# Second query group turned on TensorE: products with the identity in place of a VectorE transpose, 128-token query products, and a mask moved ahead of a division

## The chip, the cores and the metric

The kernel runs on one core of a Trainium2 chip. The metric is the device time of one execution in microseconds (us), lower is better. "The time" below is the median of the runs shown unless it says otherwise.

## The reference

Two blocks run one after the other. The first is a linear attention whose features are outer products of two 8-row sketches; the second is a two-layer network with an ELU between the layers.

```python
# q, k, v: (batch 4, heads 4, tokens 1088, 32), float32; S1, S2: (8, 32), float64
def phi(x):                                     # 64 features of a token
    a = einsum('rd,bhsd->bhsr', S1, x); b = einsum('rd,bhsd->bhsr', S2, x)
    return einsum('bhsi,bhsj->bhsij', a, b).reshape(..., 64)
kv  = einsum('bhsf,bhsd->bhfd', phi(k), v);  z = phi(k).sum(tokens)
x   = (phi(q) @ kv) / (phi(q) @ z + 1e-6)       # heads side by side: (4352, 128)
h   = x @ w_in                                  # w_in (128, 2048), float64
out = where(h > 0, h, exp(min(h, 0)) - 1) @ w_out   # w_out (2048, 128), float64
```

The weights arrive as 64-bit floats, and the kernel makes 32-bit floats of their words itself ("rounding" below).

## The kernel before

**Stages.** The 4352 tokens are cut into half tiles of 64; eight half tiles make a group of 512 tokens (groups 0 to 8). Everything up to the first product with `w_in` is the head: the keys of batch 0 are turned and sketched, key features and values are summed into `kv`, and the queries of groups 0 and 1 go through sketch, division (`q2_den`), feature products (`q2_out`), a turn on TensorE (`q4_early`) and the product with `kv` (`q5_early`), which gives `xg`, the network's input. After the head each step is one pair of 128-wide slices of the hidden layer: `mm1` (tile `h`), ELU on ScalarE (`elu_a`: RELU, then EXP) and VectorE (`elu_d`, tile `gg`), then `mm2` (tile `o`, or `pa`/`pb` where a seven-product scheme is used). Keys and queries of later batches are worked into these steps at fixed places.

**Order.** The schedule is written out by hand: each engine runs its instructions in the order in which the program text issues them, and a waiting instruction keeps those behind it on its engine waiting. Each `dma_start` on `nc.sync` goes to SP's queue in the same way.

**Rounding of a weight slice** takes `RA` (a mask on VectorE, L101), `RB` (a RELU with a scale on ScalarE, L106) and `RC` (sign L116, mantissa L120, low word L128, product L136, all on VectorE). Slices 0 and 1 are the two first `w_in` pairs, slices 2 and 3 the two first `w_out` pairs; `RC_2` treats the two `w_in` pairs in one go, and `RE` is its last step.

**Tiles and lines.** `qT` holds the queries of a batch with head dimension on the partitions: `transp` (L281) is one STREAM_TRANSPOSE on VectorE from the loaded tile `hd_q`. Half tiles 0 to 7 of batch 0 are turned first, 8 to 16 later (L974). The products that read it in the head are `q1_first` (tile `abqp`, L516), `q1z_first` (`zqp`, L528; denominators) and `q1_second` (`abwp`, L537; group 1). `KA` (`kv`, L428) sums keys and values; `KS_first` turns its result into `kvS` (L480 to L482). `q4_early` writes `qtp` (L636) and ScalarE copies it to `qpT` (L637); `q5_early` writes `xps` (L643), which ScalarE copies to `xg` (L649). `keep_warm` issues products of ones whose result (`idle`) nobody reads.

**PSUM.** Tag `h` has four banks in turn, tag `aux` two, `o0` and `o1` one each; `kv` of batch 0 lies in `o1`.

The text order just ahead of and behind the first `mm1`:

```python
    q5_early(0)
    keep_warm(1, 192, width[0])
    mm1_first()
    q2(1, 2, lambda: RA(2))
    RB(2)
    elu_a(0, 0, 0)
    elu_a(0, 0, 1, (0,))
    mm1(0, 1, (0,))
    q4_early(1)
```

Of the kernel before, what the change touches and what calls it, by code (L numbers as in the profile page):

```python
# [12 lines left out]
F32 = mybir.dt.float32  # L13
# [9 lines left out]
def _ap(ap: bass.AP, free):  # L23
    return dataclasses.replace(ap, ap=[list(ap.ap[0])] + [list(x) for x in free])
# [3 lines left out]
def kernel(  # L28
# [21 lines left out]
    nc = tc.nc  # L50
    B, H, S, D = q.shape
    R = S1.shape[0]
    P = 128
# [21 lines left out]
    def load_hd(eng, x, src, b, t0, t1, c=slice(0, 2)):  # L75
        if (x, b) not in hd:
            hd[x, b] = work.tile([P, 2, NT, D], F32, name="hd_" + x, tag="hd_" + x)
        eng.dma_start(hd[x, b][:, c, t0:t1, :],
                      src[b].rearrange("h (a c t) d -> (h a) c t d", a=32, c=2)[:, c, t0:t1, :])
# [104 lines left out]
    def RA(i):  # L184
        round_w(round_a, i)

    def RB(i):
        round_w(round_b, i)
# [23 lines left out]

    load_v(0)
    load_w(0, 0)
    load_hd(nc.sync, "q", q, 0, 8, NT)
    load_w(1, 0)
    load_w(1, 1)
    load_w(0, 1)
# [35 lines left out]
    def quarters(dst, lhs, rhs, tile=None, **kw):  # L254
        tile = tile or width[0]
        for c in range(0, P, tile):
            nc.tensor.matmul(dst[c:c + tile], lhs[:, c:c + tile], rhs, skip_group_check=True,  # L257
                             tile_position=(0, c), **kw)


    def keep_warm(n, cols=256, tile=P):
        ones = nc.const_aps.tensor(1.0, [P, 256], F32)
        for i in range(n):
            for c in range(0, P, tile):
                nc.tensor.matmul(idle[c:c + tile, :cols], ones[:, :tile], ones[:, :cols], skip_group_check=True,  # L265
                                 tile_position=(0, c))
# [13 lines left out]
    def transp(dst, x, b, t0, t1):  # L280
        nc.vector.transpose(dst[b][:, t0:t1, :].rearrange("p t (a c) -> p c t a", c=2), hd[x, b][:, :, t0:t1, :])  # L281


    SXh = const.tile([P, FD], F32, name="SXh")

    def make_SXh():
# [9 lines left out]
    SW = const.tile([FD, H, 3, R], F32, name="SW")  # L296
    SWq = const.tile([FD, B, 2, 4, R], F32, name="SWq")
    SWs = const.tile([FD, B - 1, 4, R], F32, name="SWs")
    keep_warm(3)
    keep_warm(1, 224)  # L300
    sps = psum.tile([P, 512], F32, name="sps", tag="aux")
    nc.tensor.matmul(sps[:, :2 * R], Sx[:].rearrange("p h d -> p (h d)"), ident[:, :2 * R])
    make_SXh()
# [119 lines left out]
    def KA(b):  # L423
        kv = kv_ps[b] = psum.tile([P, 512], F32, name="kv", **(dict(tag="aux") if b else dict(tag="o1", bufs=1)))
        kp = [feats.pop((b, half)) for half in range(2)]
        for i in range(KT):
            for h in range(H):
                nc.tensor.matmul(kv[32 * h:32 * h + 32, :R * R], vt[b][:, (h * KT + i) * D:(h * KT + i + 1) * D],  # L428
                                 kp[i // 5][:, i % 5, h].rearrange("p i j -> p (i j)"),
                                 start=(i == 0), stop=(i == KT - 1), skip_group_check=True, tile_position=(0, 32 * h))  # L430
            if b:
                z_tile(b, kv, i)
# [10 lines left out]

    def Z(b, ps, zl):

        quarters(ps[:, 96:128], SXh[:], zl[:], None if b else 64)

    def Z_out(b, ps):
        z = wzs[b] = SW[:, :, 2, :] if b == 0 else work.tile([FD, H, R], F32, name="wz", tag="wz")[:]
# [25 lines left out]
            z_tile(0, ps, i)  # L475
        return ps, ZC(0, ps)

    def KS_first():
        kd = work.tile([P, 2, R * R], F32, name="kd", tag="kd", bufs=1)
        nc.scalar.copy(kd[:], _ap(kv_ps[0][:, :R * R], [[0, 2], [1, R * R]]))  # L480
        nc.tensor.transpose(kv_ps[0][:, 128:256], kd[:].rearrange("p w f -> p (w f)"), ident[:])
        nc.scalar.copy(kvS[:].rearrange("p h d -> p (h d)"), kv_ps[0][:, 128:256])  # L482

# [14 lines left out]
    def half_tile(g, k):  # L498
        return divmod(8 * g + k, NT)
# [11 lines left out]
    def q1_first():  # L511
        p = psum.tile([P, 512], F32, name="abqp", tag="aux")
        for i in range(4):
            for u in range(2):
                b, t = half_tile(0, 2 * i + u)
                nc.tensor.matmul(p[64 * u:64 * u + 64, i * 64:i * 64 + 64], qT[b][:, t, :],  # L516
                                 Sab[:].rearrange("p h y -> p (h y)"),
                                 skip_group_check=True, tile_position=(0, 64 * u))
        abw[0] = work.tile([P, H * 4, 2 * R], F32, name="abq", tag="abq", bufs=1)
        nc.scalar.copy(abw[0][:].rearrange("p (h t) y -> p h t y", h=H),  # L520
                       p[:, :256].rearrange("p (t h y) -> p h t y", t=4, h=H))

    def q1z_first():
        p = psum.tile([P, 512], F32, name="zqp", tag="h", bufs=4)
        for i in range(4):
            for u in range(2):
                b, t = half_tile(0, 2 * i + u)
                nc.tensor.matmul(p[64 * u:64 * u + 64, i * 32:i * 32 + 32].rearrange("p (h r) -> p h r", h=H),  # L528
                                 qT[b][:, t, :], SW[:, :, 2, :], skip_group_check=True, tile_position=(0, 64 * u))
        return p[:, :128].rearrange("p (t h r) -> p h t r", t=4, h=H)  # L530

    def q1_second():
        p = psum.tile([P, 512], F32, name="abwp", tag="h", bufs=4)
        for i in range(4):
            for u in range(2):
                b, t = half_tile(1, 2 * i + u)
                nc.tensor.matmul(p[64 * u:64 * u + 64, i * 96:i * 96 + 96], qT[b][:, t, :],  # L537
                                 SW[:].rearrange("p h x r -> p (h x r)"), skip_group_check=True,
                                 tile_position=(0, 64 * u))
        abw[1] = work.tile([P, H * 4, 3 * R], F32, name="abw1", tag="abq1", bufs=1)  # L540
        nc.scalar.copy(abw[1][:].rearrange("p (h t) y -> p h t y", h=H),
                       p[:, :384].rearrange("p (t h y) -> p h t y", t=4, h=H))
# [49 lines left out]
    def q2(g, parts=1, between=None):  # L592
        q2_den(g, None, between)
        q2_out(g, parts)

    def q2_den(g, zq=None, between=None):
        m = H * (un[g] if g > 1 else qn[g])
        x = abw[g][:, :m, :]
        pw = pws[g % 2]
        if zq is None:  # L600
            nc.vector.tensor_mul(pw[:, :m, :R], x[:, :, R:2 * R], x[:, :, 2 * R:3 * R])
        else:
            nc.vector.tensor_mul(pw[:, :m, :R].rearrange("p (h t) r -> p h t r", h=H),
                                 x[:, :, R:2 * R].rearrange("p (h t) r -> p h t r", h=H), zq)
        if between:
            between()
        den = work.tile([P, 8 * H], F32, name="den", tag="den")
        nc.vector.tensor_reduce(den[:, :m], pw[:, :m], axis=AX, op=ADD)
        nc.vector.reciprocal(den[:, :m], den[:, :m])
        an = work.tile([P, 8 * H, R], F32, name="an", tag="an")  # L610
        nc.vector.tensor_mul(an[:, :m], x[:, :, R:2 * R], _ap(den[:, :m], [[1, m], [0, R]]))
        ans[g] = an

    def q2_out(g, parts=1, between=None):
        m = H * qn[g]
        x, an = abw.pop(g), ans.pop(g)
        qp[g] = work.tile([P, 4 * H, R, R], F32, name="qp", tag="qp", bufs=2)
        for i in range(parts):
            if i and between:
                between()  # L620
            h = slice(i * m // parts, (i + 1) * m // parts)
            a_ = an[:, h]
            b_ = x[:, h, :R]
            nc.vector.tensor_mul(qp[g][:, h], _ap(a_, list(a_.ap[1:]) + [[0, R]]),
                                 _ap(b_, [b_.ap[1], [0, R], b_.ap[2]]))

    def q4_early(g):

        qpT[g] = work.tile([P, H, 2, P], F32, name="qpT", tag="qpT", bufs=2)
        for hh in range(2):  # L630
            p = psum.tile([P, 512], F32, name="qtp", tag="aux")
            for h2 in range(2):
                for m in range(2):
                    o = (h2 * 2 + m) * P
                    r = (2 * hh + h2) * 4 + 2 * m
                    nc.tensor.transpose(p[:, o:o + P], qp[g][:, r:r + 2].rearrange("p t i j -> p (t i j)"), ident[:])  # L636
            nc.scalar.copy(qpT[g][:, 2 * hh:2 * hh + 2], p[:].rearrange("p (h m s) -> p h m s", h=2, m=2))  # L637

    def q5_early(g):
        xp = [psum.tile([P, 512], F32, name="xps", tag="aux") for _ in range(2)]  # L640
# [320 lines left out]
    Z(0, zps, zl)  # L961
    Z_out(0, zps)
    KO_first(7, KT)
    keep_warm(1, 96, 64)
    zq = q1z_first()
    q2_den(0, zq, lambda: RA(0))
    q2_out(0, 2, lambda: RA(1))
    KA(0)
    KS_first()
    keep_warm(1)  # L970
    RB(0)
    RB(1)
    q4_early(0)
    transp(qT, "q", 0, 8, NT)  # L974
    RC_2()
    RE(0)
    RE(1)
    q1_second()
    q5_early(0)
    keep_warm(1, 192, width[0])  # L980
    mm1_first()
    q2(1, 2, lambda: RA(2))
    RB(2)
    elu_a(0, 0, 0)
# [218 lines left out]
```

## Time and profile before

| | us |
|---|---|
| median of 3 runs | 265.75 |
| the 3 runs | 265.44 to 265.97 |
| the profiled execution, its own time | 265.08 |
| its span | 263.3 |
| TensorE busy | 257.8 (98%) |
| VectorE busy | 188.2 (71%) |
| ScalarE busy | 184.5 (70%) |
| GpSimd busy | 168.2 (64%) |
| first product with `w_in` begins | 15.58 |

The granted TensorE clock is 1.0 throughout. TensorE's busy share says that a product is in flight, not that the array is full. The 16 DMA engines are busy from 3 us to about 24 us of the span, at 228 to 405 GB/s in each us, and have little to do after that. Times inside the span are counted from its start; the difference between the span and the execution's own time, 1.78 us, lies around it.

### The profile page before, as it was taken

What the parts mean: (1) busy time and instruction counts of PE and PEld (TensorE: products, weight loads), DVE (VectorE), ACT (ScalarE), POOL (GpSimd) and SP (SyncE); (2) the same over time, 40 slices, a digit from 0 to 9 for tenths busy, and PEclk for the clock granted to TensorE, in tenths of its full rate; (3) what the DMA queues carried; (4) which work ended last, traced back from release to release, by engine and by line L of the source; (5) the groups of instructions that cost most, each with busy time, mean ns of one, the idle gap of its engine ahead of it and who ended that gap; (6) DMA issues with size and microseconds to landing.
All of it is one profiled execution on the core that took longest, in us unless ns stands there. A gap on an engine that the chain in (4) does not pass through costs nothing.

```text
span 263.3 us, 9739 instructions
## 1 busy us (share of the span) xinstructions
PE 257.8 (98%) x4127; PEld 160.5 (61%) x4127; DVE 188.2 (71%) x349; ACT 184.5 (70%) x356; POOL 168.2 (64%) x251
## 2 busy tenths in 40 slices
PE   8899999999999999999999999999999999999994
PEld 7652334354346756667666666665666666667994
DVE  6899999997969997996477676644446445674651
ACT  2479978677567656775587777776777777777793
POOL 4400009105477996798869799888688888998300
PEclk9999999999999999999999999999999999999999
DMA  5997099020011110000100110011001100110011
GB/s 176 339 349 209 2 277 230 1 72 18 2 24 26 26 20 2 2 4 17 31 3 0 29 18 0 2 19 25 3 2 21 23 4 0 18 20 8 2 30 32
DMA packets 26442, 13.73 MB, mean 52 GB/s; under 512 B 19328, under 2 KB 24576, under 8 KB 26400
## 3 DMA queue, kind: packets, MB, share of 16 engines
q1 hardware_dynamic: 25968, 12.76, 18.9%
q8 instruction: 32, 0.52, 0.9%
q10 hardware_dynamic: 368, 0.30, 0.3%
q0 software_dynamic: 64, 0.07, 0.1%
q14 instruction: 10, 0.08, 0.1%
HBM read 10.88 MB, written 2.23 MB: 50 GB/s over the span
## 4 chain that ended last, share of the span: by engine, by line
PE 96%; POOL 1%; DVE 1%; ACT 1%; issue 0%
PE h L257 44%; PE pb L792 16%; PE pa L792 13%; PE o L257 5%; PE pb L768 4%; PE ol L257 3%; PE idle L265 1%; PE kv L428 1%; PE h L686 1%; PE qps L686 1%; POOL kp L324 1%; PE kfps L360 1%; PE qps L576 1%; PE qtp L636 1%; PE kv L257 1%; PE abp L341 1%
## 5 line engine op out<-in xcount | busy, mean ns | idle before, releaser
L257 PE MATMUL h<-xg,W 128*32 128x512 f32 (+3 forms) x904 | 130.7, 539 | 0.4 <-ACT xg L649 0.4
L875 DVE SCALAR_TENSOR_TENSOR gg<-e,h 128x512 f32<-128x512 f32 x128 | 85.6, 683 | 54.1 <-ACT e L869 50.6
L867 ACT ACTIVATE e<-h 128x512 f32<-128x512 f32 x128 | 75.5, 590 | 45.6 <-PE h L257 42.9
L869 ACT ACTIVATE e<-e 128x512 f32<-128x512 f32 x128 | 80.9, 632 | 3.8
L257 PEld LDWEIGHTS h<-xg,W 128*32 128x32 f32 (+1 forms) x904 | 42.6, 122 | 43.2 <-issue 34.9
L754 POOL TENSOR_TENSOR tt<-gg 128x256 f32<-128x256 f32 x50 | 37.0, 741 | 16.4 <-DVE gg L875 16.1
L751 POOL TENSOR_TENSOR tt<-gg 128x256 f32<-128x256 f32 x50 | 36.7, 734 | 5.5 <-DVE gg L875 5.1
L755 POOL TENSOR_TENSOR tt<-tt,gg 128x256 f32<-128x256 f32 x50 | 37.5, 750 | 3.9
L756 POOL TENSOR_TENSOR tt<-gg,tt 128x256 f32<-128x256 f32 x50 | 37.2, 744 | 3.9
L792 PEld LDWEIGHTS pa<-gg,W 128*64 128x64 f32 (+1 forms) x496 | 23.8, 125 | 23.5 <-issue 22.9
L792 PE MATMUL pa<-gg,W 128*64 128x128 f32 (+1 forms) x496 | 30.5, 274 | 0.0
L792 PE MATMUL pb<-tt,SS 128*64 128x128 f32 (+1 forms) x480 | 29.5, 273 | 0.0
L792 PEld LDWEIGHTS pb<-tt,SS 128*64 128x64 f32 (+1 forms) x480 | 22.6, 126 | 0.0
L792 PE MATMUL pa<-tt,SS 128*32 128x128 f32 (+1 forms) x288 | 21.0, 273 | 0.0
L133 POOL TENSOR_TENSOR raw<-raw,tiny 128x512 f32<-128x512 f32 x1 | 1.0, 1044 | 29.4 <-DVE raw L128 29.4
L792 PE MATMUL pb<-tt,W 128*64 128x128 f32 (+1 forms) x256 | 19.8, 273 | 0.0
L792 PE MATMUL pb<-gg,SS 128*64 128x128 f32 (+1 forms) x256 | 19.8, 273 | 0.0
L257 PE MATMUL o<-gg,W 128*32 128x512 f32 x128 | 15.3, 594 | 0.0
L792 PEld LDWEIGHTS pa<-tt,SS 128*32 128x32 f32 (+1 forms) x288 | 13.6, 124 | 0.0
L792 PEld LDWEIGHTS pb<-gg,SS 128*64 128x64 f32 (+1 forms) x256 | 12.7, 125 | 0.0
L792 PEld LDWEIGHTS pb<-tt,W 128*64 128x64 f32 (+1 forms) x256 | 12.6, 125 | 0.0
L768 PE MATMUL pb<-gg,W 128*32 128x256 f32 x192 | 11.5, 380 | 0.0
(163 smaller groups left out, 279.5 us busy)
## 6 DMA issues: line engine op xcount, KB each, us to landing
raw<-in_moe_w_in_dram SPq DMA_DIRECT2D x8, 256.0 KB, 6.6
raw<-in_moe_w_out_dram SPq DMA_DIRECT2D x8, 256.0 KB, 6.4
hd_k<-in_k_dram SPq DMA_DIRECT2D x3, 544.0 KB, 7.3
hd_q<-in_q_dram SPq DMA_DIRECT2D x3, 544.0 KB, 7.9
out_dram<-ob SPq DMA_DIRECT2D x88, 16.0 KB, 1.5
v<-in_v_dram SPq DMA_DIRECT2D x4, 288.0 KB, 6.8
v<-in_v_dram SPq DMA_DIRECT2D x4, 256.0 KB, 8.3
hd_k<-in_k_dram SPq DMA_DIRECT2D x1, 288.0 KB, 3.3
```

The costliest lines, as they stand in the source:

```text
L257: nc.tensor.matmul(dst[c:c + tile], lhs[:, c:c + tile], rhs, skip_group_check=True, tile_position=(0, c), **kw)
L265: nc.tensor.matmul(idle[c:c + tile, :cols], ones[:, :tile], ones[:, :cols], skip_group_check=True, tile_position=(0, c))
L686: nc.tensor.matmul(ps[w][s * r:s * r + s, 64 * k:64 * (k + m)], lhs, qpT[g, i][rows, o + 2 * k:o + 2 * (k + m), f, :], start=(f == 0 and j ...
L751: nc.gpsimd.tensor_tensor(t[:, 0], b12, b11, op=SUB)
L754: nc.gpsimd.tensor_tensor(t[:, 2], b22, b12, op=SUB)
L755: nc.gpsimd.tensor_tensor(t[:, 1], t[:, 2], b11, op=ADD)
L756: nc.gpsimd.tensor_tensor(t[:, 3], b21, t[:, 1], op=SUB)
L768: nc.tensor.matmul(acc[1][0][r:r + width[0], 256 * hi:256 * hi + 256], lhs[:, w:w + width[0]], gg[:, c, 256 * u:256 * u + 256], start=(cp ...
L792: nc.tensor.matmul(bank[r:r + width[0], P * col:P * col + P], lhs[:, w:w + width[0]], rhs[:, u], start=(first and i in ((0,) if g == 1 els ...
L867: nc.scalar.activation(e, hs[g, cp][c][:, :n], RELU, scale=-1.0)
L869: nc.scalar.activation(e, e, EXP, scale=-1.0)
L875: nc.vector.scalar_tensor_tensor(gs[g, cp][:, c, :n], es[g, cp][:, c, :n], -1.0, hs[g, cp][c][:, :n], op0=ADD, op1=MAX)
```

## The change

- The load of half tiles 8 to 16 of batch 0 (one DMA into `hd_q`) becomes two DMAs into a new tile `q2s`, with the tokens on the partitions: half tiles 8 to 11 on partitions 0 to 63, 12 to 16 on 64 to 127.
- The VectorE transpose of these half tiles goes. In its place `turn_q` makes 16 products of `q2s` with the identity (four heads by four), `turn_q_out` copies them to `qT` on ScalarE in two halves, and `turn_q_last` turns the single half tile 16 by four products behind `mm1_first`, with a ScalarE copy.
- `q1_first`, `q1z_first` and `q1_second` use 128 tokens as the stationary operand in place of two times 64; `Z` of batch 0 and one `keep_warm` use 128 columns too. The other `keep_warm` calls change in size or go.
- `RA(0)` stands ahead of the division's first product in place of behind it; `RB(0)` stands ahead of `KA(0)`; `KS_first` is cut in two, and its second half stands between the halves of `q4_early(0)`.

```diff
@@ -212,7 +212,10 @@
     load_v(0)
     load_w(0, 0)
-    load_hd(nc.sync, "q", q, 0, 8, NT)
+    q2s = const.tile([P, H, 5, D], F32, name="q2s")
+    for u, t0, t1 in ((0, 8, 12), (1, 12, NT)):
+        nc.sync.dma_start(q2s[64 * u:64 * u + 64, :, :t1 - t0, :],
+                          q[0].rearrange("h (y t) d -> y h t d", t=NT)[:, :, t0:t1, :])
     load_w(1, 0)
     load_w(1, 1)
     load_w(0, 1)
@@ -259,7 +262,7 @@
     def keep_warm(n, cols=256, tile=P):
-        ones = nc.const_aps.tensor(1.0, [P, 256], F32)
+        ones = nc.const_aps.tensor(1.0, [P, 512], F32)
         for i in range(n):
             for c in range(0, P, tile):
                 nc.tensor.matmul(idle[c:c + tile, :cols], ones[:, :tile], ones[:, :cols], skip_group_check=True,
@@ -281,6 +284,28 @@
         nc.vector.transpose(dst[b][:, t0:t1, :].rearrange("p t (a c) -> p c t a", c=2), hd[x, b][:, :, t0:t1, :])
+    turned_q = []
+    def turn_q(t0, t1):
+        if not turned_q:
+            turned_q.append(psum.tile([P, 512], F32, name="qtu", tag="h", bufs=4))
+        for t in range(t0, t1):
+            for h in range(H):
+                nc.tensor.matmul(turned_q[0][D * h:D * h + D, P * t:P * t + P], q2s[:, h, t, :], ident[:],
+                                 skip_group_check=True, tile_position=(0, D * h))
+    def turn_q_out(t0, t1):
+        nc.scalar.copy(qT[0][:, 8:16, :].rearrange("p (u t) y -> p t u y", u=2)[:, t0:t1],
+                       turned_q[0][:, P * t0:P * t1].rearrange("p (t u y) -> p t u y", u=2, y=64))
+    def turn_q_last():
+        for h in range(H):
+            nc.tensor.matmul(kv_ps[0][D * h:D * h + D, 256:320], q2s[64:, h, 4, :], ident[64:, 64:],
+                             skip_group_check=True, tile_position=(64, D * h))
+        nc.scalar.copy(qT[0][:, 16, :], kv_ps[0][:, 256:320])
     SXh = const.tile([P, FD], F32, name="SXh")
     def make_SXh():
@@ -296,8 +321,7 @@
     SW = const.tile([FD, H, 3, R], F32, name="SW")
     SWq = const.tile([FD, B, 2, 4, R], F32, name="SWq")
     SWs = const.tile([FD, B - 1, 4, R], F32, name="SWs")
-    keep_warm(3)
-    keep_warm(1, 224)
+    keep_warm(2, 496)
     sps = psum.tile([P, 512], F32, name="sps", tag="aux")
     nc.tensor.matmul(sps[:, :2 * R], Sx[:].rearrange("p h d -> p (h d)"), ident[:, :2 * R])
     make_SXh()
@@ -443,7 +467,7 @@
     def Z(b, ps, zl):
-        quarters(ps[:, 96:128], SXh[:], zl[:], None if b else 64)
+        quarters(ps[:, 96:128], SXh[:], zl[:], None if b else P)
     def Z_out(b, ps):
         z = wzs[b] = SW[:, :, 2, :] if b == 0 else work.tile([FD, H, R], F32, name="wz", tag="wz")[:]
@@ -475,9 +499,12 @@
             z_tile(0, ps, i)
         return ps, ZC(0, ps)
-    def KS_first():
+    def KS_first_a():
         kd = work.tile([P, 2, R * R], F32, name="kd", tag="kd", bufs=1)
         nc.scalar.copy(kd[:], _ap(kv_ps[0][:, :R * R], [[0, 2], [1, R * R]]))
+        return kd
+    def KS_first_b(kd):
         nc.tensor.transpose(kv_ps[0][:, 128:256], kd[:].rearrange("p w f -> p (w f)"), ident[:])
         nc.scalar.copy(kvS[:].rearrange("p h d -> p (h d)"), kv_ps[0][:, 128:256])
@@ -511,11 +538,9 @@
     def q1_first():
         p = psum.tile([P, 512], F32, name="abqp", tag="aux")
         for i in range(4):
-            for u in range(2):
-                b, t = half_tile(0, 2 * i + u)
-                nc.tensor.matmul(p[64 * u:64 * u + 64, i * 64:i * 64 + 64], qT[b][:, t, :],
-                                 Sab[:].rearrange("p h y -> p (h y)"),
-                                 skip_group_check=True, tile_position=(0, 64 * u))
+            b, t = half_tile(0, 2 * i)
+            nc.tensor.matmul(p[:, i * 64:i * 64 + 64], qT[b][:, t:t + 2, :].rearrange("p t y -> p (t y)"),
+                             Sab[:].rearrange("p h y -> p (h y)"), skip_group_check=True)
         abw[0] = work.tile([P, H * 4, 2 * R], F32, name="abq", tag="abq", bufs=1)
         nc.scalar.copy(abw[0][:].rearrange("p (h t) y -> p h t y", h=H),
                        p[:, :256].rearrange("p (t h y) -> p h t y", t=4, h=H))
@@ -523,20 +548,18 @@
     def q1z_first():
         p = psum.tile([P, 512], F32, name="zqp", tag="h", bufs=4)
         for i in range(4):
-            for u in range(2):
-                b, t = half_tile(0, 2 * i + u)
-                nc.tensor.matmul(p[64 * u:64 * u + 64, i * 32:i * 32 + 32].rearrange("p (h r) -> p h r", h=H),
-                                 qT[b][:, t, :], SW[:, :, 2, :], skip_group_check=True, tile_position=(0, 64 * u))
+            b, t = half_tile(0, 2 * i)
+            nc.tensor.matmul(p[:, i * 32:i * 32 + 32].rearrange("p (h r) -> p h r", h=H),
+                             qT[b][:, t:t + 2, :].rearrange("p t y -> p (t y)"), SW[:, :, 2, :],
+                             skip_group_check=True)
         return p[:, :128].rearrange("p (t h r) -> p h t r", t=4, h=H)
     def q1_second():
         p = psum.tile([P, 512], F32, name="abwp", tag="h", bufs=4)
         for i in range(4):
-            for u in range(2):
-                b, t = half_tile(1, 2 * i + u)
-                nc.tensor.matmul(p[64 * u:64 * u + 64, i * 96:i * 96 + 96], qT[b][:, t, :],
-                                 SW[:].rearrange("p h x r -> p (h x r)"), skip_group_check=True,
-                                 tile_position=(0, 64 * u))
+            b, t = half_tile(1, 2 * i)
+            nc.tensor.matmul(p[:, i * 96:i * 96 + 96], qT[b][:, t:t + 2, :].rearrange("p t y -> p (t y)"),
+                             SW[:].rearrange("p h x r -> p (h x r)"), skip_group_check=True)
         abw[1] = work.tile([P, H * 4, 3 * R], F32, name="abw1", tag="abq1", bufs=1)
         nc.scalar.copy(abw[1][:].rearrange("p (h t) y -> p h t y", h=H),
                        p[:, :384].rearrange("p (t h y) -> p h t y", t=4, h=H))
@@ -624,7 +647,7 @@
             nc.vector.tensor_mul(qp[g][:, h], _ap(a_, list(a_.ap[1:]) + [[0, R]]),
                                  _ap(b_, [b_.ap[1], [0, R], b_.ap[2]]))
-    def q4_early(g):
+    def q4_early(g, between=None):
         qpT[g] = work.tile([P, H, 2, P], F32, name="qpT", tag="qpT", bufs=2)
         for hh in range(2):
@@ -635,6 +658,8 @@
                     r = (2 * hh + h2) * 4 + 2 * m
                     nc.tensor.transpose(p[:, o:o + P], qp[g][:, r:r + 2].rearrange("p t i j -> p (t i j)"), ident[:])
             nc.scalar.copy(qpT[g][:, 2 * hh:2 * hh + 2], p[:].rearrange("p (h m s) -> p h m s", h=2, m=2))
+            if between and hh == 0:
+                between()
     def q5_early(g):
         xp = [psum.tile([P, 512], F32, name="xps", tag="aux") for _ in range(2)]
@@ -961,24 +986,28 @@
     Z(0, zps, zl)
     Z_out(0, zps)
     KO_first(7, KT)
-    keep_warm(1, 96, 64)
+    keep_warm(1, 96)
     zq = q1z_first()
-    q2_den(0, zq, lambda: RA(0))
+    RA(0)
+    q2_den(0, zq)
     q2_out(0, 2, lambda: RA(1))
+    RB(0)
     KA(0)
-    KS_first()
-    keep_warm(1)
-    RB(0)
+    kd = KS_first_a()
+    turn_q(0, 2)
+    turn_q_out(0, 2)
+    turn_q(2, 4)
+    turn_q_out(2, 4)
     RB(1)
-    q4_early(0)
-    transp(qT, "q", 0, 8, NT)
+    q4_early(0, lambda: KS_first_b(kd))
     RC_2()
     RE(0)
     RE(1)
     q1_second()
     q5_early(0)
-    keep_warm(1, 192, width[0])
+    keep_warm(1, 128)
     mm1_first()
+    turn_q_last()
     q2(1, 2, lambda: RA(2))
     RB(2)
     elu_a(0, 0, 0)
```

## The prediction

> **What bounds the kernel now.** I read the page's chain by engine first, then the chain in order of time through the head, then ScalarE and VectorE alone in the timeline around the first products with `w_in`.
>
> The page's line:
>
> ```profile
> PE 96%; POOL 1%; DVE 1%; ACT 1%; issue 0%
> ```
>
> TensorE carries the end nearly everywhere, so whatever delays TensorE is paid in full unless it had a hole. The chain through the head (start, us, what):
>
> ```profile
> 11.01 0.69 DVE qp L624
> 11.70 0.21 DVE W L101
> 11.91 0.61 DVE qp L624
> ...
> 12.65 0.63 PE qtp L636 x4
> 13.28 0.85 PE abwp L537 x16
> 14.13 0.70 PE xps L643 x16
> 14.83 0.64 ACT xg L649 x2
> ...
> 15.58 2.79 PE h L257 x40
> 18.37 1.02 PE qtp L636 x8
> 19.39 0.99 PE h L257 x8
> 20.39 0.59 PE xps L643 x16
> 20.98 1.85 PE o L257 x16
> ```
>
> The chain sits on VectorE's query rows up to 12.5 us, then goes through the turn, `xps` and `xg` to the first `h` at 15.58, which I call T. From T on it never leaves TensorE. So the change has two accounts: what it does to T, and what it puts behind T. Next, ScalarE from the timeline (start, duration, instruction, idle before and its releaser):
>
> ```profile
> 14.81 0.65 ACT L649 COPY xg<-xps 128x256 f32<-128x256 f32 x2 [0.15 <-PE xps L643]
> 16.21 0.51 ACT L106 ACTIVATE W<-W,ebias 128x256 uint32<-128x256 uint32 x1 [0.75 <-DVE W L101]
> 17.14 0.60 ACT L867 ACTIVATE e<-h 128x512 f32<-128x512 f32 x1 [0.42 <-PE h L257]
> 17.77 0.63 ACT L869 ACTIVATE e<-e 128x512 f32<-128x512 f32 x1
> 18.30 0.58 ACT L867 ACTIVATE e<-h 128x512 f32<-128x512 f32 x1
> 18.99 1.07 ACT L637 COPY qpT<-qtp 128x512 f32<-128x512 f32 x2
> ```
>
> Between T and the first RELU ScalarE does one weight step (RB(2), L106) in its idle time; from 17.14 on it is full. And VectorE:
>
> ```profile
> 9.62 0.29 DVE L603 TENSOR_TENSOR pw<-abq,zqp 128x128 f32<-128x128 f32 x1 [0.23 <-PE zqp L528]
> 9.82 0.33 DVE L101 TENSOR_SCALAR W<-raw 128x256 uint32<-128x256 uint32 x1
> 18.43 0.69 DVE L875 SCALAR_TENSOR_TENSOR gg<-e,h 128x512 f32<-128x512 f32 x1
> 20.30 0.43 DVE L136 SCALAR_TENSOR_TENSOR W<-raw,W 128x256 f32<-128x256 f32 x1
> ```
>
> The last two tell what is late next: `gg` starts 0.03 us behind its EXP, and the rounding of the first `w_out` slice queues behind it and ends at 20.73, just ahead of the first `o` product at 20.91.
>
> **What the Trainium skill says.** "TensorE: Matmul & The Clock Gate", under the architectural detail of the array, gives ScalarE and VectorE strictly first-in-first-out queues, and lets TensorE pull only weight loads ahead, not products. The trace agrees: RB(2) ran ahead of the RELU although it had to wait 0.75 us, as in the text. "TensorEngine Tiling", Key Properties, says that a change of tiling mode drains TensorE. Here 16 `o` products take 1.85 us behind `xps` (another mode) and 1.72 us behind `h` (the same): about 0.13 us a change. "DMA: Bandwidth & Descriptors", Specifications, names 512 B as the least for line rate; the new load's rows are 512 and 640 B, the old ones 1152 B. No row here shows such a load.
>
> **Part 1: what happens to T.**
> - RA(0) moves ahead of `pw`. Now it sits between `pw` and its reduction, which start 0.45 apart; dependent rows of this size start 0.32 apart (10.07 to 10.39), so its leaving gives 0.13. Ahead of `pw` it costs its spacing, 0.20 (11.62 to 11.82), unless it fits the 0.23 us hole. Its data are the first `w_in` pair, issued at 3.90 and landing 5.7 us later, at 9.60. So it starts at 9.65, `pw` at 9.85 and the reduction at 10.17 in place of 10.07: +0.10. Landed by 9.3, it would be -0.19.
> - The VectorE transpose goes: 0.70 us of spacing (12.42 to 13.12), but it stands behind the second `qp`. Only `abwp` waited for it. `xps` needs the second `qpT` copy, ended at 13.90, so it could start at 13.95 and starts at 14.06: worth 0.11, no more. The rounding behind it comes 0.7 earlier; it was not late.
> - `turn_q`: 16 products of two passes over 128 columns. Sixteen 128x512 products, four side by side, take 1.72 us, so four of 128 columns take 0.107; 8 x 0.107 = 0.86 us, in TensorE's hole between `kv` (ends 10.64) and `qtp` (11.75), where 0.60 of idle products go. Free while the load is there: the old one had landed by about 10.4.
> - Their two copies (0.37 each as `abq`'s 256 columns) go to ScalarE: 11.2 and 11.65, then RB(1) at 12.05, `qpT` 12.50, `kvS` 13.05, second `qpT` 13.43 behind its `qtp` (0.10 late as above), end 14.02, `xps` 14.07. RB(0) ahead of `kd` fills ScalarE's 1.90 us wait there.
> - 128-token products: 8 instructions for 16. Two 64-token products of `abqp` cost 2 x 31 = 62 ns ((0.69 - 0.22) / 15 each). One of 128 costs 62 if columns set the pace, or 107 by the skill's price for a 128-column weight load (same TensorE page, LDWEIGHTS: columns over 1.2), which predicts 53 for 64 columns where the trace has 31. I take no change; at 107 it is 8 x 45 = 0.36 for `zqp`, mostly beside the RA(0) wait, and 0.18 for `abwp`.
> - One more DMA on SP. Everything in SP's queue ahead of it keeps its place; behind it, transfers land over 5 us after issue, so 0.6 us of issue is hidden. At worse efficiency the second `w_in` pair lands up to 0.4 late and RA(1), ahead of the second `qp`, waits.
> - The early `keep_warm` has 992 columns as before: nothing.
> Sum for T: +0.10 - 0.11 = 0.0; ends -0.3 and +0.5.
>
> **Part 2: what lies behind T.** `turn_q_last` is four products behind `mm1_first` on TensorE, and its copy is ScalarE's next instruction behind `xg`. In it I see the whole change: the copy cannot run before `mm1_first` is through, and RB(2), the RELU and the EXP queue behind it.
> - `mm1_first`: 32 x 0.054 = 1.72. Change of mode 0.14, 8 passes of 64 columns, four side by side, 2 x 0.054 = 0.11, tail 0.2: result at T+2.17, copy at T+2.20.
> - Copy of 64 columns: between 0.19 (32 columns) and 0.27 (128), spacing 0.17. RB(2) at T+2.37 in place of idle time, spacing 0.46 (0.91 for a pair). First RELU at T+2.83; now 17.14 = T+1.56. **1.27 us late.**
> - EXP T+3.46 to 4.09, `gg` T+4.12, and RC(2) ends as now 2.30 behind `gg`'s start: T+6.42. First `o` at T+6.47; now 20.91 = T+5.33. **+1.14.**
> - The same over `qpT`: second RELU T+3.99, copies T+4.50 and 4.98, end 5.57, `xps` T+5.62 against T+4.74; `o` could start at T+6.2. So the mask chain ends last.
> - TensorE alone would lose 0.11 + 2 x 0.14 = 0.39; that lies inside the 1.14.
> - TensorE has no hole behind that (`h` 3.43 for 32, `o` 1.72 for 16), so nothing gives it back.
>
> **Sum:** 0.0 + 1.14 against the profiled execution, 265.08 + 1.14 = 266.2. That execution lies 0.67 under the median of 265.75, so the median should be **266.9**. No change is what lies within 0.2%, 0.53 us, about what a measurement of this kernel can tell.
>
> **Rivals.**
> - *The hold is covered* (0.15). TensorE has `mm1` (0.86), `qtp` (1.02) and `mm1` (0.99) between `turn_q_last` and `xps`. If these 2.9 us cover ScalarE, only TensorE's 0.39 stays: 266.1, not slower by what can be told. It decides if `qpT` ends by T+5.0 and the rounding by T+5.7; my rows say 5.6 and 6.4.
> - *VectorE sets T* (0.06, faster). For it: VectorE is 0.9 to 1.0 busy from 10 to 16 us, and the first weight pair is rounded at 15.43, 0.03 from `xg` at 15.46. If T moves by 0.70 + 0.19 and the hold is covered, -0.89 + 0.39 = -0.5: 265.2. It needs `xg` at 14.6, but `qp` to `qtp` to `qpT` alone keep `xps` at 13.7 or later, so T at 15.2. Against it, then.
> - *Late rows too* (0.15). Short rows land the second half late and wide weight loads cost 107 ns: T + 0.5 on top, 267.4.
> - *Main case* (0.64): 266.5 to 267.3.
> Faster 0.06; same 0.15 and 0.04 of the main case's low edge, 0.19; slower 0.75. The range, 266.0 to 267.6, takes in the covered case and most of the late one.
>
> **What would show it.** ScalarE's timeline: a long wait of the 64-column copy on TensorE (about 2 us), then RB(2), then the RELU near T+2.8. A TensorE hole ahead of `xps` and `o`, chain through ACT and DVE there. T within 0.3 of 15.6. Wrong if the RELU still starts near T+1.6, or T is under 15.0.

## The result, and the profile after

The changed kernel takes 267.17 us (median of 6 runs, 267.11 to 267.78), against 265.70 (265.44 to 265.97) for the kernel before beside it: ratio 1.0063, 95% interval 1.0051 to 1.0076. The profiled execution takes 267.11, its span is 265.3. The profiled execution of before, 265.08, was the quickest of all its runs shown, so between the two profiles there are 2.0 us, between the medians 1.5.

The page's chain by engine:

```profile
PE 95%; DVE 2%; ACT 1%; issue 0%
```

The chain in order of time through the head of the changed kernel (start, us, what):

```profile
8.80 0.20 PE zps L260 x2
...
9.28 1.08 PE zqp L552 x8
10.36 1.14 PE kv L452 x72
11.50 0.48 PE qtu L296 x16
...
12.00 0.38 ACT qT L300
...
12.43 0.69 PE qtu L296 x16
...
13.14 0.37 ACT qT L300
13.51 0.42 ACT W L106
...
13.95 0.70 DVE W L116
...
16.45 1.93 PE h L260 x32
18.39 0.29 PE kv L305 x8
...
18.70 0.21 ACT qT L307
18.91 0.41 ACT W L106
19.32 0.50 ACT e L892
...
20.50 0.69 DVE gg L900
...
22.36 0.44 DVE W L136
...
22.84 1.92 PE o L260 x16
```

T, the first `h`, has gone from 15.58 to 16.45, and behind it the chain leaves TensorE for the last turn's copy, RB(2), RELU, EXP, `gg` and the rounding of the first `w_out` slice: the path that the prediction wrote out. The first `o` starts at 22.84 in place of 20.91. ScalarE in the timeline:

```profile
15.83 0.65 ACT L674 COPY xg<-xps 128x256 f32<-128x256 f32 x2 [0.24 <-PE xps L668]
18.70 0.21 ACT L307 COPY qT<-kv 128x64 f32<-128x64 f32 x1 [2.22 <-PE kv L305]
18.81 0.51 ACT L106 ACTIVATE W<-W,ebias 128x256 uint32<-128x256 uint32 x1
19.22 0.59 ACT L892 ACTIVATE e<-h 128x512 f32<-128x512 f32 x1
```

The 64-column copy waits 2.22 us for TensorE with RB(2) and the RELU behind it; RB(2)'s data had been there since 17.05, when its mask on VectorE ended. The RELU starts at T+2.77. So there are two accounts again: 0.87 us in the head, 1.06 behind T. In the head the chain does not run through the query rows any more, as it did before: `h` waits for the rounding of the first `w_in` pair, which begins at 13.95 behind the two copies of the turned queries and RB(1); before it began at 13.12.

### The profile page after: what moved, and what is told of

Its sections match the earlier page's. It is cut to its first block, busy times and chain, and to the rows that moved or that the text cites. A ratio compares the mean times of both kernels' runs of the same rounds, so it can differ in the third digit from the quotient of the medians.

```text
span 265.3 us, 9742 instructions
## 1 busy us (share of the span) xinstructions
PE 260.1 (98%) x4127; PEld 161.2 (61%) x4127; DVE 187.6 (71%) x348; ACT 184.9 (70%) x359; POOL 168.0 (63%) x251
## 4 chain that ended last, share of the span: by engine, by line
PE 95%; DVE 2%; ACT 1%; issue 0%
PE h L260 43%; PE pb L817 16%; PE pa L817 13%; PE o L260 5%; PE pb L793 4%; PE ol L260 3%; PE kv L452 2%; PE idle L268 1%; PE h L711 1%; PE qps L711 1%; PE kfps L384 1%; PE qps L599 1%; PE abp L365 1%; PE kv L260 1%; DVE raw L128 0%; PE qtu L296 0%
```

## Experiments

Times are medians, each beside runs of the kernel before on the same chip. "T" and "`o` behind T" are from each kernel's own timeline.

| kernel | us | before beside it | ratio (95%) | T | `o` behind T |
|---|---|---|---|---|---|
| before | | | | 15.58 | 5.33 |
| after | 267.17 | 265.70 | 1.0063 (1.0051 to 1.0076) | 16.45 | 6.39 |
| copy_late | 266.81 | 265.47 | 1.0052 (1.0040 to 1.0064) | 16.68 | 5.72 |
| last_early | 266.43 | 265.47 | 1.0049 (1.0031 to 1.0068) | 16.55 | 5.34 |
| narrow | 268.33 | 265.47 | 1.0104 (1.0091 to 1.0117) | 17.50 | 6.39 |
| wide_alone | 266.27 | 265.47 | 1.0031 (1.0019 to 1.0043) | 16.45 | 5.33 |
| pad_before | 266.59 | 265.42 | 1.0054 (1.0038 to 1.0070) | 16.71 | 5.33 |
| narrow_4 | 266.60 | 265.42 | 1.0046 (1.0033 to 1.0059) | 15.76 | 6.37 |
| narrow_4_early | 265.57 | 265.42 | 1.0006 (1.0000 to 1.0013) | 16.26 | 5.33 |
| mask_move | 265.70 | 265.42 | 1.0006 (0.9997 to 1.0015) | 16.02 | 5.33 |
| hold_alone | 266.61 | 265.36 | 1.0048 (1.0034 to 1.0062) | 15.65 | 6.38 |

Theory: ScalarE's queue stands behind the last turn's copy (1.06 us; called the hold), and the wide products make T late. Rivals: the loss behind T is only TensorE's own extra work; T is late from the turn on TensorE and its copies.

**copy_late: only the copy elsewhere.**

```diff
     RE(3)
     elu_d(0, 1, 1)
+    turn_q_last_out()      # the ScalarE copy, taken out of turn_q_last
```

> The copy of the last half tile is taken out of ScalarE's queue between xg and the first RELU and put behind the ELU of the second pair; its four products stay behind the first w_in products. Hold theory (ScalarE's queue stands behind that copy): the first RELU comes back from T+2.8 to about T+1.6, and only TensorE's own 0.39 us of turn and mode changes stays, so the first o product comes at about T+5.7 in place of T+6.4: 0.7 us under the changed kernel, 266.5. Rival (the copy's place is harmless, TensorE's extra products or the head cost the time): no gain, 267.1 to 267.2.

The RELU goes back to T+1.56 and `o` to T+5.72, the step as expected (chain):

```profile
18.61 0.25 PE kv L305 x8
18.86 0.99 PE h L260 x8
```

Behind the turn's products the chain now stays on TensorE, and what is left over 5.33 is 0.39 us, as much as the prediction put on the products with their two mode changes (changes of the way in which TensorE's array is split into tiles). So of the 1.06 us, 0.67 come from the place of the copy. The time fell by only 0.36 where 0.7 was expected. T was 0.23 later in this execution, of which 0.15 were there before the query products began (a copy of `abk` starts at 7.22 here, at 7.07 in the changed kernel).

**last_early: products and copy ahead of the first `h`.**

```diff
-    keep_warm(1, 128)
-    mm1_first()
     turn_q_last()
+    mm1_first()
```

> The turn of the last half tile, products and copy, goes ahead of the first w_in products, in the place of the idle products there. Hold theory: RELU at about T+1.6, no mode change inside the w_in products, first o product at about T+5.4: 1.0 us under the changed kernel, 266.1, and 0.3 to 0.4 less than with the copy alone moved. Rival (the loss is all in the head before T): 267.1.

`o` comes at T+5.34, as in the kernel before: the whole 1.06 us is the place of the products and their copy together. The runs spread from 266.11 to 267.91, so the timeline says more than the median; the profiled execution took 266.13, 1.0 less than the changed kernel's.

**hold_alone: the kernel before with the hold added.**

```diff
     mm1_first()
+    for h in range(H):
+        nc.tensor.matmul(kv_ps[0][D * h:D * h + D, 256:320], ident[64:, D * h:D * h + D], ident[64:, 64:], ...)
+    nc.scalar.copy(hold[:], kv_ps[0][:, 256:320])
```

> The kernel before with one thing added: four products of 64 columns behind the first w_in products and a ScalarE copy of their result (identity slices, into a tile that nobody reads), at the place where the change has its last turn. Hold theory: the head and T stay, RELU comes at T+2.8 in place of T+1.6, the first o product at T+6.4 in place of T+5.3: 1.0 to 1.1 us over before, 266.4 to 266.6. Rival (the hold costs only where the head is late already): only TensorE's own 0.4, 265.8.

```profile
17.89 0.21 ACT L986 COPY hold<-kv 128x64 f32<-128x64 f32 x1 [2.36 <-PE kv L984]
18.41 0.59 ACT L867 ACTIVATE e<-h 128x512 f32<-128x512 f32 x1
```

T is nearly where it was (15.65), the RELU comes at T+2.76 and `o` at T+6.38, 1.05 later; the median is 1.25 us longer. The hold costs the same in an undisturbed head; the rival of 0.4 us is out.

**wide_alone: the kernel before with 128-column products.**

```diff
-            for u in range(2):
-                nc.tensor.matmul(p[64 * u:64 * u + 64, i * 64:i * 64 + 64], qT[b][:, t, :], ..., tile_position=(0, 64 * u))
+            nc.tensor.matmul(p[:, i * 64:i * 64 + 64], qT[b][:, t:t + 2, :].rearrange("p t y -> p (t y)"), ...)
         # the same in q1z_first, q1_second, Z of batch 0 and the idle product behind it
```

> The kernel before with nothing changed but the 128-column products (abqp, zqp, abwp, z's turn, and the idle products behind it). Weight-load theory: SW 0.4 and pw 0.8 us later, xg and T 0.7 to 0.9 later, 266.4 to 266.6. Rival (the wide products cost nothing, as 8 instructions stand for 16): 265.7.

As expected: 0.80 us slower, T at 16.45, and here the chain runs through `zqp`, `pw`, the query rows and `xg`. TensorE of the changed kernel shows the price of such products:

```profile
7.69 1.10 PE L542 MATMUL abqp<-Sab,qT 128*128 128x64 f32 x8
9.28 1.08 PE L552 MATMUL zqp<-SW,qT 128*128 128x32 f32 x8
14.04 1.03 PE L561 MATMUL abwp<-SW,qT 128*128 128x96 f32 x8
```

One takes 0.28 us (0.27 for `abwp`), so the spacing is (1.10 - 0.28) / 7 = 117, then 114 and 108 ns, for 64, 32 and 96 columns moved. It does not follow the moved columns. It lies close to the price for a 128-column weight load that the prediction quoted from the Trainium skill ("TensorE: Matmul & The Clock Gate", LDWEIGHTS), 107 ns; that the weight load sets it is inferred from this. Two 64-column products of `abqp` had cost 62.

**narrow: the changed kernel with 64-column products.**

```diff
# the reverse of wide_alone, on the changed kernel
-            nc.tensor.matmul(p[:, i * 64:i * 64 + 64], qT[b][:, t:t + 2, :].rearrange("p t y -> p (t y)"), ...)
+            for u in range(2):
+                nc.tensor.matmul(p[64 * u:64 * u + 64, i * 64:i * 64 + 64], qT[b][:, t, :], ..., tile_position=(0, 64 * u))
```

> The changed kernel with all query products of the head, the turn of z and the idle products behind it on 64 columns again. Weight-load theory (a product with a 128-column stationary operand takes about 110 ns whatever it moves, two of 64 columns 62): abqp and zqp are through in about 0.7 us each in place of 1.1, SW comes 0.4 and pw 0.8 us earlier; then the landing of the first w_in pair and RB(1) on ScalarE hold part of it, so T comes 0.5 to 0.8 earlier: 266.4 to 266.7. Rival (T is late from the turn on TensorE and its copies on ScalarE, not from the products): T earlier by 0.2 at most, 267.0.

Wrong: 1.2 us slower, not faster. TensorE's timeline:

```profile
13.93 0.46 PE L564 MATMUL abwp<-SW,qT 128*64 128x96 f32 x5
15.68 0.71 PE L564 MATMUL abwp<-SW,qT 128*64 128x96 f32 x11 [1.29 <-issue]
```

`zqp` is early as expected (8.98 against 9.28), but in the middle of `abwp`, with all operands there, TensorE stands for 1.29 us, and the releaser is "issue": it waited for nothing that the profile shows. Counting the products ahead of the stop gives 220. In last_early TensorE also stops behind product 220, for 0.41 us, between the products of the last turn. New theory: TensorE runs out of fetched instructions there. Another gap must be kept apart from this one: in every kernel with idle products behind `xps`, their weight load comes 0.41 us late with the releaser "issue". That gap goes with the idle products and not by count: it lies behind product 221 in the kernel before, but behind 193 in wide_alone (before 15.79 us), and narrow has it besides the stop (before 16.92 us). Its cause is open.

VectorE's timeline of narrow tells one thing more:

```profile
13.74 0.69 DVE L116 SCALAR_TENSOR_TENSOR W<-raw,W 128x512 uint32<-128x512 uint32 x1 [0.86 <-ACT W L106]
15.66 0.76 DVE L136 SCALAR_TENSOR_TENSOR W<-raw,W 128x256 f32<-128x256 f32 x2
```

In the changed kernel T comes 0.57 us behind the start of this last rounding step (15.88), for which `h` waits there. By the same distance T could not have come before 16.23 here, stop or no stop. By this estimate the rival holds as well: with the turn and its two copies ahead of RB(1), the narrow products alone bring T back by 0.22 us at most, not by 0.5 to 0.8. Two paths of nearly the same length lead to the late T, the query rows behind the wide products and the rounding behind the turn's copies.

**pad_before: 30 more products in the kernel before, in nearly the same time.**

```diff
     KS_first()
-    keep_warm(1)
+    keep_warm(4, 8, 32)
```

> The kernel before, with the idle product behind the turn of kv (2 instructions, 0.43 us) replaced by 16 idle products of 8 columns on 32-column tiles (32 instructions, about 0.5 us): 30 more TensorE products, hardly more time. Instruction-supply theory (with the DMA engines full, TensorE runs out of fetched instructions at about its 220th product, and stands until the next block has come, which ends between 14.6 and 16.3 us in the traces so far): product 220 is now the first of abwp in place of an idle one, so abwp begins 1.0 to 1.5 us late without any wait on an engine, and the time is 266.5 to 267.0. Rival (the 1.29 us stop seen in abwp with narrow products came from the turned queries or from chance): 265.4 to 265.6, no change.

```profile
13.36 0.38 PE L537 MATMUL abwp<-SW,qT 128*64 128x96 f32 x2
14.72 0.87 PE L537 MATMUL abwp<-SW,qT 128*64 128x96 f32 x14 [0.98 <-issue]
```

The stop lies behind product 221, now two into `abwp`, and costs T 1.1 us. The stops begin at 13.74, 14.39 and 15.87 us in pad_before, narrow and last_early, so their place is set by the count of TensorE's instructions, not by the time and not by the turned queries. This is shown. In the kernel before, a stop behind product 221 can't be told from the gap of 0.41 us ahead of the idle products. That the cause is the fetch of instructions is inferred: the first packet of the instruction queue in the DMA records ends at 13.34 us in pad_before, 14.44 in narrow and 14.82 in last_early, and TensorE goes on 1.38, 1.24 and 1.45 us later. In wide_alone that packet ends at 14.65 and product 220 comes only at 17.35, inside `h`: there is no stop. The DMA engines move 365 to 376 GB/s in each us from 12 to 16 in narrow; that an emptier DMA queue would shorten the stop was not tried.

**narrow_4: fewer products ahead of the stop.**

```diff
-            for h in range(H):
-                nc.tensor.matmul(turned_q[0][D * h:D * h + D, P * t:P * t + P], q2s[:, h, t, :], ident[:], ...)
+            nc.tensor.transpose(turned_q[0][:, P * h:P * h + P], q2s[:, h, :4, :].rearrange("p t d -> p (t d)"), ident[:])
         # with the 64-column products of narrow
```

> The changed kernel with 64-column products as in narrow, and the turn of the eight half-tile pairs by 4 full transposes of contiguous slices in place of 16 products of two passes: 28 products fewer ahead of q1_second. The slices mix head and half tile, so the queries of group 1 are put in a wrong order. Instruction-supply theory: the stop moves back from abwp to the idle products; T comes from 17.5 to 15.7 to 16.1 (RB(1) and the weight rounding then set it), the hold of ScalarE's queue behind T stays at 1.06: 266.4 to 266.8, 1.6 to 1.9 under narrow. Rival (the stop belongs to the 64-column products themselves or to the data): 268.0 or more.

Product 220 is now the first of the two idle products, which start 0.42 us apart where they start 0.27 apart in the changed kernel, so little of the stop is left. T is at 15.76, and the time 1.7 us under narrow. The wide products, costly as they are, save the same 28 instructions and so keep the stop out of the way of the changed kernel's `abwp`. This run also made the turn shorter: its copies come at 11.55 and 12.45 (12.00 and 13.14 in the changed kernel), so RB(1) and the rounding come earlier as well. It does not tell what a turn of 16 products costs.

**narrow_4_early: the same, with the last turn early.**

```diff
-    keep_warm(1, 128)
-    mm1_first()
     turn_q_last()
+    mm1_first()
```

> As narrow_4 (the queries of group 1 in a wrong order), and the last half tile's turn goes ahead of the first w_in products. If the three terms are separate (wide products or the instruction stop in the head, the hold of ScalarE's queue), the hold's 1.06 us goes as well: 265.4 to 265.8, the time of the kernel before, and the VectorE transpose that was removed has brought nothing. Rival (the removed transpose is worth its 0.7 us once the rest is mended): 264.8.

With the hold, the wide products, the stop and the 16-product turn away the time is that of the kernel before within 0.13%. The profiled execution, 265.8, is one of the slower ones: its chain begins with the second of the two new loads, which landed at 11.47, so that TensorE waited 0.74 us for it, and runs through the short turn, its copies, RB(1) and the rounding to T = 16.26. The first mask waited 0.80 us for its own landing there. So taking the VectorE transpose out and turning on TensorE in its place brings no gain; the transpose's own worth was not measured alone.

**mask_move: only the first weight steps moved.**

```diff
-    q2_den(0, zq, lambda: RA(0))
+    RA(0)
+    q2_den(0, zq)
...
+    RB(0)
     KA(0)
     KS_first()
     keep_warm(1)
-    RB(0)
```

> The kernel before with nothing changed but the order: the first mask RA(0) ahead of the division's product, RB(0) ahead of the keys' and values' products. Prediction's step: RA(0) has to wait for its landing at about 9.6 us, so pw starts 0.2 later and the reduction 0.1 later; T within 0.1 of before: 265.4 to 265.7. Rival (the mask fits the hole ahead of pw): reduction 0.1 to 0.2 earlier, 265.2 to 265.4, hardly to be told apart by time, but by the trace.

```profile
9.89 0.32 DVE L101 TENSOR_SCALAR W<-raw 128x256 uint32<-128x256 uint32 x1 [0.34 <-DMA raw<-in_moe_w_in_dram]
```

The mask waits for its landing, as predicted, and `pw` starts at 10.13, behind it. But the data landed at 9.86 in place of 9.60, and the reduction came at 10.51 in place of 10.07: T was 0.44 later in this execution, of which 0.18 were there at the first query product, where at most 0.1 was expected. In the median it is no difference that can be told. The mask waited for its landing in each kernel with this order and 64-column products (0.25 to 0.80 us), so no gain from this part was seen.

None of these runs points to a version that beats the kernel before.

## Why the prediction was right, and where it was not

- **The hold (part 2): right in mechanism and size.** Predicted against measured behind T: copy 2.20 and 2.25, RELU 2.83 and 2.77, `gg` 4.12 and 4.05, `o` 6.47 and 6.39. That is 1.06 us where 1.14 was said, with the rounding of the first `w_out` slice ending last, as said. TensorE's own share, 0.39, was met by copy_late. hold_alone shows it in the kernel before.
- **T: wrong, in two steps.** Said 0.0 with ends of -0.3 and +0.5; measured +0.87. The first step is "128-token products: I take no change". They cost 108 to 117 ns where I took 62, close to the quoted price. I had also laid `zqp`'s extra beside the RA(0) wait and overlooked `abqp`: the turn of z is queued behind it on TensorE, so `SW` was 0.43 late (9.03 against 8.60) and `pw` 0.84 (10.46 against 9.62). wide_alone shows that this alone gives T = 16.45.
- **The turn in TensorE's hole, "free": the second step.** The copies were put at 11.2 and 11.65 and came at 12.00 and 13.14; RB(1), put at 12.05, came at 13.40. The second half of the turn waited 0.49 us for the copy of the first, which shares its PSUM tile, and RB(1) stood behind both copies. The rounding, said to come 0.7 earlier, began 0.83 later and set T. In narrow, with the narrow products back, it would still have held T at 16.23 or later, by the estimate given there. So each of the two steps alone makes T late, by 0.87 and by about 0.65; they run side by side and do not add.
- **RA(0), +0.10:** the wait is right, but mask_move measured +0.44 at the reduction. In the changed kernel `pw` was so late that the mask ran at 9.73 in its hole and cost nothing. The -0.19 for an early landing doesn't come out of the prediction's own rows: with `pw` where it was, only the 0.13 is left. No run had such a landing.
- **The VectorE transpose, worth 0.11 at most:** not contradicted. narrow_4_early shows no gain, but it has the turn in its place.
- **The in-order queue:** RB(2) ahead of the RELU, quoted as agreement, proves little, as the RELU's data weren't there yet. The changed kernel shows it: RB(2), ready at 17.05, began at 18.81, behind the copy.
- **The sum:** 266.9 said, 267.17 measured, and in part that is luck. Against the profiled executions the shift is 2.03 us where 1.14 was said, because the head was put at nothing. The prediction then added 0.67 to come from the profile to the median, and the profiled execution of the changed kernel lies only 0.06 under its median. The two errors, 0.89 too little and 0.61 too much, nearly cancel.
- **The rivals:** the covered case is out. It needed `qpT` to end by T+5.0 and the rounding by T+5.7; they ended at T+5.46 and T+6.35. Of the late case, the wide loads came true. The rows did land late, at 10.96 in narrow, where TensorE waited 0.32 us for them, against about 10.4 for the old load; but that half was issued at 5.20 in place of 4.55 and landed 5.8 us behind its issue, as the old load did, so short rows are not shown to be the reason. The changed kernel reached them at 11.31 and did not wait.

## What to carry to other kernels

Where an engine's queue runs in order, ask of each new instruction what it waits for and what is queued behind it: a copy of 0.2 us that must wait for TensorE, with its four products, cost 1.06 us, 0.67 of them because the RELU stood behind the copy, and nothing behind T when both stood a line further up. Price a product of few moved columns by its stationary columns too: one product with 128 of them took 108 to 117 ns here, where two with 64 had taken 62. When a part of a change is called free because its engine has a hole, follow what stands behind it on the other engines as well. And before adding or removing many small TensorE instructions in a stretch with full DMA engines, look for "issue" gaps in the timeline and count where they fall.

## What was not expected of the hardware

TensorE stands still in the head behind product 220 or 221, whatever that product is: 0.98 us in pad_before, 1.29 in narrow, 0.41 in last_early. Its place goes by count. It stops only where that product comes early enough (none at 17.35 in wide_alone), and in last_early it cost nothing, as `h` had to wait for the rounding anyway. And products with a 128-column stationary operand kept 108 to 117 ns apart for 32, 64 and 96 moved columns alike.
